# Half of the spectral modes folded in early, and a last stage that contracts 64 rows

## The chip, the cores and the metric

One Trainium2 chip, one of its cores. The time is that of one execution on the device, in microseconds (us); of the kernel before, three runs gave a median of 456.17 us. Engines: TensorE (PE, with its weight loads PEld), VectorE (DVE), ScalarE (ACT), GpSimd (POOL), and SyncE (SP), which here only issues DMAs.

## The reference

Two parts in a row. Batch 8, 8 heads of 64, sequence 576, model width 512, 64 modes.

```python
proj = einsum('bhsd,df->bhsf', x, w_phi); proj -= max(abs(proj))   # for q and for k
phi  = concatenate([exp(proj), exp(-proj)])
num  = phi_q @ (phi_k.T @ v);  den = phi_q @ sum(phi_k)
x    = (num / den)                        # [8, 576, 512] after the heads are joined
X    = rfft(x, axis=1)[:, :64]
Y    = X_m @ (w_r[m] + i w_i[m])          # for each of 64 modes a 512x512 complex matrix
y    = irfft(Y, n=576)
u    = x + y
out  = u + relu(u @ w_ch)
```

The weights w_r and w_i are 64 x 512 x 512 in f32 each, 134 MB in all.

## The kernel before, in words

**Attention stage.** 32 steps, each one pair of batches or heads, make x, kept in `xs_all` (8 batches x 5 chunks of up to 128 tokens, bf16), and its forward transform, kept transposed in `XT`. Beside them the weights of the modes stream in: 32 groups of 8 modes by a quarter of the width (the first 8 groups: 16 modes by an eighth), each a `wr` and a `wi` tile cast to bf16 by the DMA that POOL issues (`weights`, L162). Three tiles of each stand ready (`NW = 3`), so group k+2 is issued once the products of group k-1 are done. `mode_mm` makes a group's products (L416), `mode_sum` adds them into `Yacc`. Groups 0 to 21 run within the attention stage; its last six steps also turn and multiply the first six chunks of x by w_ch (`flip_early`, `times_w_early`, into `xw0`).

**The tail of the stream, groups 22 to 31.** The order of instructions is written by hand and each engine works through its own in that order. Groups 24 to 31 complete the sums of 8 modes each, for all batches. Each of them sums its products to `yst` (L444), turns them (`ptY`, L805) and copies them to `sY` (L806). After every second group, `by_batch` makes for 16 modes and all batches Z = Y w_ch and Y itself, rows by mode (`psZY`, L705 and L711, on the PSUM tags T0 and T1), and copies them to `zy` (L718): mode rows 32 P to 32 P + 31 hold P = 0 to 3, real and imaginary parts. For P below 3 the copies are put in a list, `copies`, and taken from it one by one by `pieces`; for P = 3, after group 31, one batch of each half is copied and the other six go through a staging tile `st` (L735) and DMAs (L737, SP and POOL).

Between groups, `pieces(n)` (numbers by group in `plan`) does n times: turn two chunks of x (`flip_x`, PSUM tag T3, copied to `sT` by DVE, L657) and multiply the two turned before by w_ch (`times_w`, PSUM tag T2, L665, copied to `xw` by ACT, L667). `reordered` puts 11 pairs of chunks of `xs_all` in the order of tokens in which the output is written, in place (L692, L694, tags T0 and T1). A PSUM tile on a tag can be written only when all that read the previous tile on this tag have done so.

**The last stage.** 20 units: for each b of 0 to 3 the chunk pairs (b,0), (b,2), (b+4,0), (b+4,2) and one unit with the half chunks 4 of b and b+4. Each has two PSUM tiles, psB and psA, on T2 and T3 or, every other unit, on T0 and T1. psB takes x w_ch (L753, `add_xw`) and Z times the inverse transform `CI` (L760, `add_z`, 128 rows: real and imaginary parts of 64 modes); ACT takes the Relu of it into the output tile `of` (L762). psA takes x (L768, `add_x`) and Y times `CI` (L774, `spec`); DVE adds it (L776). In 11 units, called late, x is not added on PE but by POOL at the end (L780). SP issues the outputs (L856): those of a late unit three units later. The first unit's `add_xw` stands ahead of group 31's products.

The names of the rows in the profile are those of these tiles.

Of the kernel before, what the change touches and what calls it, by code (L numbers as in the profile page):

```python
# [21 lines left out]
NCH = 5  # L22
# [4 lines left out]
def kernel(  # L27
# [31 lines left out]
    N_EARLY = 6  # L59
# [4 lines left out]
    CI = const.tile([128, NCH, 128], BF16, name="CI")  # L64
# [310 lines left out]
    def flip_early(i):  # L375
        pt = psum.tile([128, 4, 128], BF16, name="pte", tag="tx", bufs=1)
        for dc in range(4):
            nc.tensor.transpose(pt[:, dc, :], xs_all[:, i, dc * 128:(dc + 1) * 128], ident_b)
        sT = pa_mid.tile([128, 4, 128], BF16, name="sTe", tag="sTe", bufs=1)
        nc.vector.tensor_copy(sT, pt)  # L380
        return sT

# [7 lines left out]
    def mode_mm(k, tag="yr"):  # L390
        g, gi = groups[k]
        XT = XTs[1 - g if k < 8 else g % 2]
        wt = W.pop(k)
# [16 lines left out]
        psY = psum.tile([128, DMODEL], F32, name="psY", tag=tag, bufs=1)  # L410
        for ri in range(2):
# [95 lines left out]
    def inverse_matrix(c):  # L507
# [12 lines left out]
        o, i = CI[:, c, :], pct  # L520
        if c < 4:
            o, i = o.rearrange("r (p j) -> r j p", j=2), i.rearrange("r (j p) -> r j p", j=2)
        nc.vector.tensor_scalar_mul(out=o, in0=i, scalar1=coefcol)
# [117 lines left out]
    zy = pb.tile([128, 2, B_, DMODEL], BF16, name="zy", bufs=1)  # L641
    zall, yall = zy[:, 0], zy[:, 1]
    xw = pb.tile([128, B_ * NCH - N_EARLY, DMODEL], BF16, name="xw", bufs=1)


    todo = list(range(N_EARLY, B_ * NCH, 2))
# [3 lines left out]
    def flip_x(i):  # L650
        pt = psum.tile([128, 2, 4, 128], BF16, name="pt", tag="T3")
        for x in range(2):
            for dc in range(4):
                nc.tensor.transpose(
                    pt[:, x, dc, :], xs_all[:, i + x, dc * 128:(dc + 1) * 128], ident_b)
        sT = pb.tile([128, 2, 4, 128], BF16, name="sT", tag="sT", bufs=3)
        nc.vector.tensor_copy(sT, pt)  # L657
        ahead.append((i, sT))

    def times_w():  # L660
        i, sT = ahead.pop(0)
        ps = psum.tile([128, 2, DMODEL], F32, name="psW", tag="T2")
        for x in range(2):
            for dc in range(4):
                nc.tensor.matmul(ps[:, x, :], lhsT=sT[:, x, dc, :], rhs=wchb[:, dc, :],  # L665
                                 start=(dc == 0), stop=(dc == 3))
        nc.scalar.copy(xw[:, i - N_EARLY:i + 2 - N_EARLY, :], ps)  # L667

    def pieces(n):
        for _ in range(n):  # L670
# [4 lines left out]
            if len(ahead) > 1:  # L675
                times_w()
# [4 lines left out]
    late = {0: ((0, 2), (1, 0), (1, 2)), 1: ((0, 0), (1, 0), (1, 2)),  # L681
            2: ((0, 0), (1, 0), (1, 2)), 3: ((0, 0), (0, 2))}
    reorder = sorted((b + 4 * x) * NCH + c for b in range(4) for x, c in late[b])

    def reordered(tag):
        i = reorder[0]
        if todo and i + 2 > todo[0]:
            return
        reorder.pop(0)
        ps = psum.tile([128, 2, DMODEL], F32, name="psX", tag=tag)  # L690
        for x in range(2):
            nc.tensor.matmul(ps[:, x, :], lhsT=ident_p, rhs=xs_all[:, i + x, :],  # L692
                             start=True, stop=True)
        nc.scalar.copy(xs_all[:, i:i + 2, :], ps)  # L694


    def by_batch(sY, P):
# [17 lines left out]
        rows = slice(32 * P, 32 * P + 32)  # L715

        def copy(j, h, eng):
            eng(zy[rows, :, j + 4 * h, :], ps[h][32 * j:32 * j + 32])  # L718

        if P < 3:  # L720
            for h in range(2):
                mm_z(h)
                mm_r(h)
            copies.extend([lambda j=j: (copy(j, 0, nc.scalar.copy),
                                        copy(j, 1, nc.vector.tensor_copy)) for j in range(4)])
# [4 lines left out]
        for h, eng in ((0, nc.scalar.copy), (1, nc.vector.tensor_copy)):  # L730
            mm_z(h)
            mm_r(h)
            copy(0, h, eng)
            st = pb.tile([128, 2, DMODEL], BF16, name=f"st{h}", bufs=1)
            eng(st, ps[h])  # L735
            for j in range(1, 4):
                (nc.sync if j == 1 else nc.gpsimd).dma_start(  # L737
                    zy[rows, :, j + 4 * h, :], st[32 * j:32 * j + 32])

    def parts(u):
        for x, (b, c) in enumerate(u["bc"]):
            if u["half"]:
                yield slice(64 * x, 64 * x + 64), 0, b, c, ident_b[:, 0:64], CI[:, c, 0:64]
            else:
                yield slice(0, 128), x, b, c, ident_p, CI[:, c, :]

    def add_xw(u):
        u["psB"] = ps = psum.tile([128, 2, DMODEL], F32, name="psB", tag=u["tags"][0])  # L750
        for r, x, b, c, idn, ci in parts(u):
            i = b * NCH + c
            nc.tensor.matmul(ps[r, x, :], lhsT=idn,  # L753
                             rhs=xw0[:, i, :] if i < N_EARLY else xw[:, i - N_EARLY, :],
                             start=True, stop=False)

    def add_z(u):
        ps = u["psB"]
        for r, x, b, c, idn, ci in parts(u):
            nc.tensor.matmul(ps[r, x, :], lhsT=ci, rhs=zall[:, b, :],  # L760
                             start=False, stop=True)
        nc.scalar.activation(u["o"], ps[:, 0, :] if u["half"] else ps, ACT.Relu)  # L762

    def add_x(u):
        u["psA"] = ps = psum.tile([128, 2, DMODEL], F32, name="psA", tag=u["tags"][1])
        if not u["late"]:
            for r, x, b, c, idn, ci in parts(u):
# [3 lines left out]
    def spec(u):  # L771
        ps, late, o = u["psA"], u["late"], u["o"]
# [114 lines left out]
```

## Time and profile before

| | |
|---|---|
| Median of 3 runs (lowest, highest) | 456.17 us (455.78, 456.91) |
| Span of the profiled execution | 456.7 us |
| PE busy, share of the span | 301.7 us, 66% |
| DVE | 292.0 us, 64% |
| ACT | 261.8 us, 57% |
| POOL | 198.8 us, 44% |
| DMA moved | 97.70 MB, mean 214 GB/s |
| Products of group 31, wi half, start | 416.08 us |
| Last DVE addition ends | 449.85 us |

The span is that of one execution under the profiler, from its first to its last instruction; it is 0.5 us above the median of the runs. In the page's slices each digit is the busy share of a fortieth of the span (11.4 us) in tenths. A row of the order of time gives start, duration, engine, line and operation, the tiles written and read, and in brackets how long the engine had been idle and what ended that. Matmuls overlap: a row of eight is shorter than eight of one. PEclk is the clock that TensorE was granted, as a share of full speed.

### The profile page before, as it was taken

Reading aid. Unit: us, or ns where it says so; the run is one execution under the profiler, and the core shown is the slowest. Engines: PE = TensorE matmul, PEld = TensorE weight load, DVE = VectorE, ACT = ScalarE, POOL = GpSimd, SP = SyncE. Lnnn points to the kernel's source line nnn. Section 1 sums busy time; section 2 is a strip of 40 time slices with the busy share of each in tenths; the row PEclk is TensorE's granted clock in tenths of the full one; section 3 lists DMA queues with packets and bytes.
Section 4 is the critical chain, followed back from the end, with each engine's and each line's share of the span. In section 5 each row is a group of like instructions: output and inputs, shape, how many; then the busy total and the mean of one; then the engine's idle time right before and its main releaser. Section 6 shows DMA issues by size and latency. Waiting matters only on the chain.

```text
span 456.7 us, 11065 instructions
## 1 busy us (share of the span) xinstructions
PE 301.7 (66%) x4637; PEld 197.6 (43%) x4637; DVE 292.0 (64%) x418; ACT 261.8 (57%) x528; POOL 198.8 (44%) x251
## 2 busy tenths in 40 slices
PE   3476776833767677655555544755578878868993
PEld 2355565622555565544333432433344445433341
DVE  6578789844988779876666472776322273653873
ACT  4576887833686877865545452765334455644662
POOL 3956476445563256553435231443021212100993
PEclk9976899876886769998778595999999999998997
DMA  6999999999999999999999999999999999990697
GB/s 179 195 228 222 225 213 226 221 206 216 221 228 217 230 219 222 224 219 229 218 207 217 218 218 218 207 203 207 207 207 207 207 207 207 207 179 11 223 341 299
DMA packets 84417, 97.70 MB, mean 214 GB/s; under 512 B 3152, under 2 KB 77136, under 8 KB 84368
## 3 DMA queue, kind: packets, MB, share of 16 engines
q0 software_dynamic: 75728, 76.75, 101.1%
q1 hardware_dynamic: 8480, 20.19, 12.8%
q8 instruction: 36, 0.59, 0.5%
q14 instruction: 13, 0.11, 0.1%
q10 hardware_dynamic: 160, 0.07, 0.1%
HBM read 163.64 MB, written 9.44 MB: 379 GB/s over the span
## 4 chain that ended last, share of the span: by engine, by line
DMA 34%; issue 24%; DVE 17%; PE 11%; POOL 7%; ACT 3%; SPq 1%; DVEq 0%; POOLq 0%; ACTq 0%
DMA wi<-in_moe_w_i_dram 29%; DVE mkq L233 6%; DMA wr<-in_moe_w_r_dram 4%; DVE xs_all L336 2%; DVE nd L322 2%; DVE tB L315 2%; POOL vaug L270 2%; PE ptr L184 1%; PE psNB L305 1%; ACT AA L240 1%; PE kvz L286 1%; PE psB L753 1%; DVE of L776 1%; SPq L122 1%; POOL wr L162 1%
## 5 line engine op out<-in xcount | busy, mean ns | idle before, releaser
L270 POOL TENSOR_TENSOR vaug<-vn,ee 128x576 bf16<-128x576 f32 x64 | 72.7, 1155 | 63.3 <-ACT ee L255 50.2
L240 ACT ACTIVATE AA<-psT 128x1024 bf16<-128x1024 f32 x64 | 62.0, 1021 | 43.6 <-PE psT L208 43.1
L262 ACT ACTIVATE e<-mkq 64x4 f32<-64x4 f32 (+1 forms) x128 | 26.3, 206 | 61.5 <-DVE mkq L233 59.2
L244 ACT ACTIVATE AA<-psk 128x1024 bf16<-128x1024 f32 x64 | 61.4, 1010 | 0.0
L162 POOL DMA_DIRECT2D wr<-in_moe_w_r_dram x24 | 21.9, 912 | 86.6 <-PE psY L416 77.8
L416 PEld LDWEIGHTS <-XT 128*32 128x32 bf16 x384 | 17.1, 171 | 56.6 <-issue 46.4
L667 ACT CAST xw<-psW 128x1024 bf16<-128x1024 f32 x17 | 17.2, 1013 | 40.5 <-PE psW L665 34.6
L233 DVE TENSOR_REDUCE mkq<-psk 128x8 f32<-128x1024 f32 x32 | 38.8, 1213 | 0.7 <-PE psk L199 0.7
L233 DVE TENSOR_REDUCE mkq<-psq 128x8 f32<-128x1024 f32 x32 | 38.9, 1217 | 0.4 <-PE psq L199 0.4
L435 DVE TENSOR_TENSOR Yacc<-psY,Yacc 128x512 f32<-128x512 f32 x16 | 11.0, 689 | 42.5 <-PE psY L416 42.5
L416 PE MATMUL psY<-wi,XT 128*32 128x512 bf16 x192 | 18.0, 435 | 28.8 <-DMA wi<-in_moe_w_i_dram 28.8
L286 PE MATMUL kvz<-vaug,AA 64*128 64x65 bf16 x1152 | 29.2, 210 | 11.5 <-POOL vaug L275 9.8
L190 DVE COPY kT<-ptr 128x640 bf16<-128x640 bf16 x32 | 15.7, 492 | 32.5 <-PE ptr L184 32.5
L665 PE MATMUL psW<-wchb,sT 128*128 128x512 bf16 x136 | 33.5, 391 | 2.1 <-ACT xw L667 2.1
L315 DVE TENSOR_TENSOR tB<-psNB,e 128x650 f32<-128x650 f32 x32 | 26.7, 833 | 11.2 <-PE psNB L305 10.6
L305 PEld LDWEIGHTS <-AA 128*128 128x128 bf16 x640 | 29.0, 110 | 9.3 <-issue 8.9
L286 PEld LDWEIGHTS <-AA 64*128 64x128 bf16 x1152 | 25.1, 107 | 15.9 <-issue 11.8
L162 POOL DMA_DIRECT2D wi<-in_moe_w_i_dram x24 | 21.1, 880 | 23.8 <-PE psY L416 20.5
L322 DVE TENSOR_TENSOR nd<-psNA,tB 128x650 f32<-128x650 f32 x32 | 26.7, 835 | 4.1 <-DVE tB L315 0.5
L416 PE MATMUL psY<-wr,XT 128*32 128x512 bf16 x192 | 17.0, 424 | 18.0 <-DMA wr<-in_moe_w_r_dram 8.7
L336 DVE TENSOR_TENSOR xs_all<-nd,rden 128x640 bf16<-128x640 f32 x32 | 28.0, 874 | 1.1
L184 PE MATMUL ptr<-ident_b,k 128*128 128x128 bf16 x160 | 17.9, 257 | 14.8 <-DVE qT L190 12.6
(132 smaller groups left out, 705.4 us busy)
## 6 DMA issues: line engine op xcount, KB each, us to landing
wr<-in_moe_w_r_dram POOLq DMA_DIRECT2D x24, 1024.0 KB, 25.8
wi<-in_moe_w_i_dram POOLq DMA_DIRECT2D x24, 1024.0 KB, 29.4
wr<-in_moe_w_r_dram POOLq DMA_DIRECT2D x16, 512.0 KB, 15.9
wi<-in_moe_w_i_dram POOLq DMA_DIRECT2D x16, 512.0 KB, 19.6
out_dram<-of SPq DMA_DIRECT2D x16, 512.0 KB, 3.8
vn<-in_v_dram SPq DMA_DIRECT2D x24, 288.0 KB, 5.8
q<-in_q_dram POOLq DMA_DIRECT2D x12, 288.0 KB, 19.3
k<-in_k_dram POOLq DMA_DIRECT2D x12, 288.0 KB, 20.0
```

Of the source, the lines that this page charges most:

```text
L162: nc.gpsimd.dma_start(t, w[8 * gi:8 * gi + 8, g * 128:(g + 1) * 128, :].rearrange("m p e -> p m e"))
L233: nc.vector.tensor_reduce(out=o, in_=i, axis=AX.X, op=ALU.max, apply_absolute_value=True)
L240: nc.scalar.activation(AA[:, 0, ab, 0:1024].rearrange("f (x j p) -> f j x p", j=2, p=64), st["psT"].rearrange("f j (x p) -> f j x p", p=64 ...
L244: nc.scalar.activation(AA[:, 1, ab, 0:1024].rearrange("p (c j f) -> p j c f", c=4, j=2), st["psk"], ACT.Exp, scale=sc)
L270: nc.gpsimd.tensor_tensor(out=vaug[:, ab, :, 0:64], in0=st["v"], in1=ee[:, ab, :].unsqueeze(2).to_broadcast([128, 9, D_]), op=ALU.mult,)
L286: nc.tensor.matmul(kvz[:, hh, ab * 65:(ab + 1) * 65], lhsT=AA[r, 1, ab, 128 * j:128 * j + 128], rhs=vaug[r, ab, j, :], start=(j == 0), sto ...
L305: nc.tensor.matmul(p[:, hh, 65 * c:65 * c + 65], lhsT=AA[:, 0, ab, x:x + 128], rhs=kvzF[:, hh, ab * 65:(ab + 1) * 65], start=True, stop=True,)
L315: nc.vector.tensor_tensor(out=tB, in0=st["psNB"], in1=e2.unsqueeze(3).to_broadcast([128, 2, NCH, 65]), op=ALU.mult,)
L322: nc.vector.tensor_tensor(out=nd, in0=st["psNA"], in1=st["tB"], op=ALU.add)
L336: nc.vector.tensor_tensor(out=xo, in0=nd[:, :, :, 0:64], in1=rden.to_broadcast([128, 2, NCH, 64]), op=ALU.mult,)
L416: nc.tensor.matmul(psY[32 * j:32 * j + 32, :], lhsT=XT[:, c0:c0 + 32, m], rhs=wt[ri][:, 2 * j + par, :], start=(par == 0 and ri == 0), sto ...
L665: nc.tensor.matmul(ps[:, x, :], lhsT=sT[:, x, dc, :], rhs=wchb[:, dc, :], start=(dc == 0), stop=(dc == 3))
```

## The change

The sum over modes is split: modes 0 to 31 (P = 0 and 1, complete after group 27) and modes 32 to 63.

- `zy` becomes two tiles, `zys[0]` for the low and `zys[1]` for the high modes; in each, rows 0 to 63 hold Z and rows 64 to 127 hold Y. `CI` becomes two tiles, `CIs[0]` and `CIs[1]`, with the 64 rows of its modes in both halves of the partitions. The copies of `by_batch` are 32 x 512 instead of 32 x 1024, twice as many; the DMAs after group 31 are twelve instead of six.
- `pre` is new. For each of the 11 late units it adds to x w_ch the low modes of Z, to x (put in the order of tokens) the low modes of Y, and copies both back in place, by ACT and DVE. It runs three times in group 28, three in 29, four in 30, and once inside group 31, between the wr and the wi half of its products. `reordered` is gone.
- `times_w(lo=True)`, in groups 28 to 30, adds the low modes of Z to four more pairs of chunks.
- In the last stage each unit contracts the 64 rows of the high modes, Z into psB and Y into psA in turn; units that have not had their low modes get them there. The first unit's x w_ch, x and low modes stand inside group 31 as well.
- x w_ch is kept in the order of tokens: the copies of the turned x (`sT`, `sTe`) write with a step of two elements (`copy_in_order`). The half chunks of b and b+4 share one tile.
- All copies left in `copies` are done at the end of each group's `pieces`; `plan` has one piece more in groups 24 and 29 and one less in group 30.

```diff
+    EARLY = [0, 1, 2, 3, NCH, NCH + 1]
...
+    def copy_in_order(sT, pt):
+        nc.vector.tensor_copy(sT.rearrange("d c (p j) -> d c j p", j=2),
+                              pt.rearrange("d c (j p) -> d c j p", j=2))
...
-        nc.vector.tensor_scalar_mul(out=o, in0=i, scalar1=coefcol)
+        for x in range(2):
+            r = slice(64 * x, 64 * x + 64)
+            for y in range(2):
+                o, i = CIs[x][64 * y:64 * y + 64, c, :], pct[r, :]
...
+                nc.vector.tensor_scalar_mul(out=o, in0=i, scalar1=coefcol[r, :])
...
+    def times_w(lo=False):
...
+        if lo:
+            for x, (b, c) in enumerate(chunks_of(u)):
+                o, n = (ps[64 * x:64 * x + 64, 0, :], 64) if c == 4 else (ps[:, x, :], 128)
+                nc.tensor.matmul(o, lhsT=CIs[0][0:64, c, 0:n], rhs=zys[0][0:64, b, :],
+                                 start=False, stop=True)
+            lo_z.add(u)
...
+    def pre(n):
+        for _ in range(n):
+            b, c = pre_todo.pop(0)
+            i = b * NCH + c
+            tags = ("T0", "T1") if pre_done[0] % 2 == 1 else ("T2", "T3")
+            pre_done[0] += 1
+            psb = psum.tile([128, 2, DMODEL], F32, name="psPB", tag=tags[0])
+            psa = psum.tile([128, 2, DMODEL], F32, name="psPA", tag=tags[1])
+            for x in range(2):
+                nc.tensor.matmul(psb[:, x, :], lhsT=ident_b, rhs=xw_of(b, c)[:, x, :],
+                                 start=True, stop=False)
+            for x in range(2):
+                nc.tensor.matmul(psa[:, x, :], lhsT=ident_p, rhs=xs_all[:, i + x, :],
+                                 start=True, stop=False)
+            for x in range(2):
+                for y, ps in enumerate((psb, psa)):
+                    r = slice(64 * y, 64 * y + 64)
+                    nc.tensor.matmul(ps[:, x, :], lhsT=CIs[0][r, c + x, :], rhs=zys[0][r, b, :],
+                                     start=False, stop=True)
+            nc.scalar.copy(xw_of(b, c), psb)
+            nc.vector.tensor_copy(xs_all[:, i:i + 2, :], psa)
...
-            copies.extend([lambda j=j: (copy(j, 0, nc.scalar.copy),
-                                        copy(j, 1, nc.vector.tensor_copy)) for j in range(4)])
+            copies.extend([lambda j=j: (copy(j, 0, 0, act), copy(j, 0, 1, act),
+                                        copy(j, 1, 0, dve), copy(j, 1, 1, dve)) for j in range(4)])
...
+        mm_z(0)
+        mm_r(0)
+        copy(0, 0, 0, act)
+        copy(0, 0, 1, dve)
+        act(st[0], ps[0])
+        mm_z(1)
+        mm_r(1)
+        copy(0, 1, 1, dve)
+        dve(st[1], ps[1])
+        copy(0, 1, 0, act)
...
+    def add_modes(u, lo):
+        for r, x, b, c, idn, cs in parts(u):
+            for y, (nm, done) in enumerate((("psB", lo_z), ("psA", lo_y))):
+                k = slice(64 * y, 64 * y + 64)
+                if lo and u["u"] in done:
+                    continue
+                nc.tensor.matmul(u[nm][r, x, :], lhsT=CIs[1 - lo][k, c, cs],
+                                 rhs=zys[1 - lo][k, b, :],
+                                 start=(y == 1 and not lo and u["late"]), stop=not lo)
...
-        plan = {22: 3, 23: 3, 24: 2, 25: 2, 26: 2, 27: 1, 28: 2, 29: 1, 30: 1, 31: 0}
+        plan = {22: 3, 23: 3, 24: 3, 25: 2, 26: 2, 27: 1, 28: 2, 29: 2, 30: 0, 31: 0}
+        pre_plan = {28: 3, 29: 3, 30: 4, 31: 0}
...
-            if k == 31:
+            if k < 31:
+                psY = mode_mm(k, "T3")
+            else:
+                psY = mode_mm(k, "T1", ris=(0,))
+                pre(1)
                 add_xw(u0)
-            yst = mode_sum(k, mode_mm(k, "T3"), pb)
+                add_x(u0)
+                add_modes(u0, True)
+                mode_mm(k, psY=psY, ris=(1,))
+            yst = mode_sum(k, psY, pb)
...
-            pieces(plan[k])
-            if k <= 24 or k % 2 == 0:
-                assert not copies
-                for tag in ("T0", "T1"):
-                    if reorder:
-                        reordered(tag)
-            if k == 30:
-                times_w()
+            pieces(plan[k], k >= 28)
+            while copies:
+                copies.pop(0)()
+            pre(pre_plan.get(k, 0))
...
                 if n:
                     add_xw(u)
-                add_z(u)
-                if n:
                     add_x(u)
-                spec(u)
+                    add_modes(u, True)
+                add_modes(u, False)
+                last(u)
```

`last` takes the Relu of psB by ACT, adds psA by DVE and, in a late unit, x by POOL, as before.

## The prediction

> **What bounds the kernel now.** I read the page's slices, then the engines' order of time from 330 us on, then busy time by stretch, then the groups with their shapes kept apart.
>
> ```profile
> span 456.7 us, 11065 instructions
> PE   3476776833767677655555544755578878868993
> ...
> DMA  6999999999999999999999999999999999990697
> ```
>
> The transfer engines are full from slice 2 to slice 36, about 411 us: up to there the weight stream sets the time, and what the attention stage gains or loses is absorbed. Two things follow the stream: the joint around mode group 31, and the last stage.
>
> ```profile
> 386.57 2.44 DVE L718 CAST zy<-psZY 32x1024 bf16<-32x1024 f32 x2
> 386.59 0.68 PE L416 MATMUL psY<-wr,XT 128*32 128x512 bf16 x8 [0.78 <-DVE sT L657]
> ```
>
> (both, and the next, from the order of time: start, us, engine, line, operation)
>
> ```profile
> 410.29 0.59 PE L692 MATMUL psX<-xs_all,ident_p 128*128 128x512 bf16 x2 [1.79 <-ACT zy L718]
> 410.72 3.22 PE L665 MATMUL psW<-wchb,sT 128*128 128x512 bf16 x8
> 415.04 0.59 PE L753 MATMUL psB<-xw,ident_p 128*128 128x512 bf16 x2 [1.10 <-ACT xw L667]
> 415.56 0.69 PE L416 MATMUL psY<-wr,XT 128*32 128x512 bf16 x8
> 416.08 0.60 PE L416 MATMUL psY<-wi,XT 128*32 128x512 bf16 x8
> ```
>
> The last weights were issued at 388.44 and land 26.0 us later, at 414.4; group 31's wi half starts at 416.08. So PE's queue, in order, is only 1.6 us behind the stream: groups 28, 29 and 30 start at 386.59, 395.22 and 402.78. The 410.29 line shows what makes this queue late: a PSUM tile on T0/T1 waits until the copies into zy have read the previous one.
>
> ```profile
> 448.02 1.23 DVE L776 TENSOR_TENSOR of<-psA,of 128x1024 f32<-128x1024 f32 x1 [0.46 <-ACT of L762]
> 449.17 0.68 DVE L776 TENSOR_TENSOR Yacc<-psA,Yacc 128x512 f32<-128x512 f32 x1
> ```
>
> In the last stage PE is busy 27.37 of the 29.4 us from 420.6 to 450, POOL works through 11 late units of 2.13 us from 425.50 to 449.45, the last DVE addition ends at 449.85, and the output drains until 456.7.
>
> **Prices**, from groups by shape and from the order of time:
>
> ```profile
> L657 DVE COPY sT<-pt 128x1024 bf16<-128x1024 bf16 x17 | 11.8, 692 | 20.9 <-PE pt L654 20.8
> L718 DVE CAST zy<-psZY 32x1024 bf16<-32x1024 f32 x13 | 15.8, 1219 | 2.8 <-PE psZY L711 2.5
> L388 ACT CAST xw<-psWe 128x512 bf16<-128x512 f32 x6 | 3.5, 586 | 5.3 <-PE psWe L386 5.2
> L776 DVE TENSOR_TENSOR Yacc<-psA,Yacc 128x512 f32<-128x512 f32 x4 | 2.7, 681 | 0.0
> ```
>
> ```profile
> 156.42 0.39 PE L208 MATMUL psT<-qT,w 64*128 64x512 bf16 x2 [2.09 <-DVE mkq L233]
> 424.95 0.59 PE L753 MATMUL psB<-xw,ident_p 128*128 128x512 bf16 x2
> ```
>
> A 512-column product costs 0.216 (eight in 1.89, 0.16 of it latency). Two that contract 64 rows in different halves end after 0.39, two full ones after 0.59: the halves run together, so a z/y pair costs one 0.216. A change of operand shape costs 0.11 (the gap between 426.24 and 426.34). A copy out of PSUM costs by columns, not rows: 512 take 0.585 on ACT and 0.685 on DVE, 1024 take 1.02 and 1.22.
>
> **The strided copies.** sT is now written with step 2. No row shows that from PSUM in bf16; bounds are 0.69 (contiguous, as now) and 1.22 (1024 columns in f32). I take 1.22: the only strided bf16 copy, ident_p's (SBUF to SBUF), took 231 ns for 128 columns, and less the 59 ns of a one-column memset that is 1.34 ns a column, against (692 - 425) / 512 = 0.52 for contiguous sT and sY. The Trainium skill (VectorE: DVE Perf Modes, What auto-detection actually checks) says that packing two results a cycle needs 16-bit data with step 1; by it the copy is 1.22, and no row here shows it. At 0.69 the sum is 2.7 us lower.
>
> **Up to group 28.** The four inverse-matrix writes for one (five times some 0.8 us of DVE, at 112 to 148 us) and the wider early copies lie under the stream, but the last three early copies (0.27 each) do not: +0.8. Groups 22 to 27 lose four places with two reorderings (0.96 of PE each, -3.8), gain a third piece in group 24 (+2.98, the distance of the xw copies at 345.00 and 347.99), and four strided copies nothing covers (4 x 0.53 = +2.1). Group 28 starts at 386.6 + 2.1 = 388.7. Weights 31 are issued right after it, when the queue still holds data to 404.6: the stream stays whole.
>
> **Groups 28 to 31**, the heart. A pre step is 2 products with xw, 2 with x, 2 pairs and 2 shape changes: 6 x 0.216 + 0.22 = 1.51 us of PE, ACT 1.02 and DVE 1.22 behind it; two pairs of PSUM tags alternate, so PE sets the pace. What PE waits for, group by group:
>
> Group 28: DVE has just ended sT and now does eight 0.685 copies (5.5) before it may sum group 28; the added z product of the first times_w waits for them too. Sum 0.69 and the turn to sY 0.92: at +7.0 the first flip can go. Flip, strided copy and the next flip, all through T3: at +9.4. times_w with its z product 2.45, ACT's copy 1.05 frees T2: +12.9. Three pre steps 4.5, and T3 free after the last DVE copy, 1.45: 18.9 us, where it took 8.6.
>
> Group 29: mode products, times_w, sum and sY to +4.4; by_batch 2 x 1.18 to +6.7; flip and strided copy to +8.7; eight copies 5.5 to +14.2. The next pre step is on T0/T1, the tags of these copies: PE has nothing to do for some 7 us. The rest of that step and two more: 18.3 us, where it took 7.6.
>
> Group 30: mode products and the last times_w 3.4, ACT frees T2 at +4.65, four pre steps 6.05, T1 free after 1.4: 12.1 us. Group 31: wr half 0.5, a pre step 1.5, its copies 1.45, the first unit's products 1.4: wi starts 4.8 later.
>
> Sum 18.9 + 18.3 + 12.1 + 4.8 = 54.1, so the wi half starts at 442.8, not 416.08: **+26.7 us**. The weights have been there for 28 us; DVE and PSUM tags now set the pace.
>
> **The last stage.** In wi-half time, the first addition starts 7.0 us on, as before: the copies are shorter, but the two halves of one psZY are read in turn by ACT and DVE. The second unit's addition ends at +10.45 (before +9.3): its y pair needs T1, which ACT's copy of batch 4 frees last. The 12 sends (5 on SP, 7 on POOL, 0.56 each there) end by +10.5 and cost nothing: POOL's first late addition is only then ready. From there the order of products matters. add_z stood ahead of what waits for psA; now z and y go in turn, so z's second half, the Relu and the addition all wait for the addition two units back. One round: late unit 0.06 + 0.43 + 0.19 + 1.03 + 0.02 + 1.24 = 2.97; one with x and low y (0.86 + 0.11 more) 3.94; a half unit 2.43. The odd units after the second (5 late, 2 full, 2 half) take 14.9 + 7.9 + 4.9 = 27.6. The last addition ends at 442.8 + 10.45 + 27.6 = 480.9, where it ended at 449.85. **+31.0 us** in all; PE work falls from 28 to some 25 us but does not bind. The end keeps its 6.85 us, since POOL and the output have slack.
>
> **The clock**, by busy time in stretches (PE, PEld, DVE, ACT, POOL, then granted clock, DMA share, GB/s):
>
> ```profile
> 410.00:411.00 1.00, 0.71 (x4) 0.35 (x4) 0.99 (x2) 0.32 (x2) 0.00 (x0) 1.00 0.62 103
> 411.00:412.00 1.00, 1.00 (x4) 0.34 (x3) 0.73 (x1) 0.93 (x1) 0.00 (x0) 0.56 0.38 62
> 412.00:413.00 1.00, 1.00 (x4) 0.42 (x3) 0.00 (x0) 0.00 (x0) 0.00 (x0) 0.50 0.17 28
> ```
>
> After some 3 us with transposes alone, PE ran at half clock from 411 to about 414.2: eight products took 3.22 instead of 1.89, and 3.2 us at half speed are 1.6 us of work. The waits in groups 28 and 29 are longer (6 and 7 us nearly without products) and pre steps follow both: 2 x 1.6 = **+3.2 us**. The Trainium skill (TensorE: Matmul & The Clock Gate, What's actually happening) states that an idle window of about 3.4 us halves the clock and a busy one restores it; the trace agrees, and by its figure the term would be an estimated 2 x 1.7.
>
> **Sum.** Span 456.7 + 31.0 + 3.2 = 490.9. The span is 0.5 above the median of the runs, 456.17, and I carry the difference: **490.4 us**.
>
> **Rivals.**
> *Faster:* pre steps fit under the stream and the stream's end stays the pace. For it: PE has idle time in each group before, and 11 reorderings go. wi then starts at 414.4 (-1.6); the second addition ends at 424.9, POOL's 11 x 2.13 = 23.4 from there end at 448.3 instead of 449.45, and the last output, no longer behind a late addition on SP, gains another 1.5 at most: 453.6. It decides if groups 28 to 31 take 25.7 us from 388.7 instead of 54.1. Against it: PE's own work in them, with no wait at all, is 11.5 + 11.0 + 9.7 + 3.5 = 35.7. Chance 0.03; another 0.02 for within 0.3%, about 1.4 us, which is also what a measurement of this kernel can tell from no change.
> *PE's work alone:* copies and tags get out of the way, and only those 35.7 us count. wi starts at 424.4 (+8.3), the last stage costs 0 to 4.3: about 466. Against it: the order of each queue is fixed, and before, too, PE waited for zy (410.29). Chance 0.08.
> *Halves one after the other:* if z and y of a pair do not overlap, each pair costs 0.43. Two in each of 11 pre steps and the first unit, 12 x 0.43 = 5.2, and on the odd units' rounds one product in a late and two in any other, 5 x 0.22 + 4 x 0.43 = 2.8: 498.4. For it: the pairs write two PSUM tiles that other engines have just read; against it the 0.39 row. Chance 0.11.
> *Clock low to the end:* the last stage leaves PE idle about a third of the time. If it runs at half clock there, late rounds grow by 0.43, full ones by 1.3, half ones by 0.4: 5 x 0.43 + 2 x 1.3 + 0.8 = 5.6, and with one more closing in groups 30 and 31 (1.6) 497.6. The attention stage, with PE 60 to 80% busy, shows both 1.00 and 0.53. Chance 0.11.
> The forecast keeps 0.65.
>
> **How the numbers follow.** The forecast's own range is 484 (copies at 0.69 -2.7, no closing of the clock -3.2) to 494 (both waits cost double at half clock, +3.2). The rivals above it reach 499, two of them part way together 502. Below, the case of PE's work alone is left out but for copies that partly overlap (half of the 24 us between 466 and 490): 478. Left out are the cases up to 466 (0.13) and some of the upper end (0.05). Faster 0.03, same 0.02, slower 0.95.
>
> **What would show it.** Right: group 29's products start near 407.6, group 30's near 426, group 31's wi half near 443 with the weights landed at 414 to 417; PE waits for DVE's or ACT's zy copies for 5 us or more twice; the pre steps lie 1.5 us apart; additions of late units two apart lie 3.0 us apart; granted clock under 1 after the waits. Wrong: group 31 waits for its weights (then the faster rival), or the last stage ends within 33 us of the wi half (then the order of z and y does not matter), or sT copies of 0.69.

## The result, and the profile after

The changed kernel takes **496.46 us** (median of four runs, 494.05 to 497.34), against 456.22 us (455.78 to 456.91) for the kernel before on the same chip: 1.086 times as long, 95% interval 1.082 to 1.089. Its profiled execution took 497.34 us, with a span of 495.5.

The page of the changed kernel: its slices are 12.4 us each.

```profile
span 495.5 us, 11304 instructions
...
PE   2558677447675776774747377457875858497883
...
DMA  6999999999999999999999999999999993000687
```

Before, the transfer engines were full to slice 36 and empty in one slice. Now the stream of weights ends at about 414 us, where it ended before, and three slices are empty. The wi half of group 31 starts 38 us after the last weights have landed, so the transfers hide nothing of this stretch any more.

What PE waits for from group 28 on, in its order of time (start, us, engine, line, operation, idle time before it and what ended that), with one of DVE's two stretches of copies ahead of it:

```profile
393.64 5.61 DVE L780 CAST zy<-psZY 32x512 bf16<-32x512 f32 x8
398.58 0.59 PE L710 MATMUL psW<-zy,CI 64*128 64x512 bf16 x2 [1.97 <-DVE zy L780]
...
404.35 3.11 PE L705 MATMUL psW<-wchb,sT 128*128 128x512 bf16 x8
...
415.02 0.69 PE L423 MATMUL psY<-wr,XT 128*32 128x512 bf16 x8 [1.35 <-DVE xs_all L753]
...
425.47 0.38 PE L742 MATMUL psPB<-xw,ident_b 128*128 128x512 bf16 x1 [3.13 <-ACT zy L780]
429.19 1.03 PE L745 MATMUL psPA<-xs_all,ident_p 128*128 128x512 bf16 x2 [3.35 <-DVE zy L780]
...
447.52 0.68 PE L423 MATMUL psY<-wr,XT 128*32 128x512 bf16 x8 [1.35 <-DVE xs_all L753]
...
452.30 0.70 PE L423 MATMUL psY<-wi,XT 128*32 128x512 bf16 x8
```

Group 28 starts at 393.66, group 29 at 415.02, group 30 at 435.50, the wr half of group 31 at 447.52 and its wi half at 452.30, where the kernel before has 386.59, 395.31, 402.78, 415.56 and 416.08. Groups 28 and 29 take 21.4 and 20.5 us instead of 8.7 and 7.5. In both, PE stands behind DVE's or ACT's copies out of psZY: 2.0 us in group 28, and 3.1 and 3.4 us in group 29 with one product between. After both the clock is low. Two of the stretches that show it (busy us of PE, PEld, DVE, ACT, POOL, then granted clock, DMA share, GB/s):

```profile
402.00:404.00 2.00, 0.62 (x7) 0.45 (x5) 1.29 (x1) 0.00 (x0) 0.00 (x0) 0.50 1.24 206
428.00:430.00 2.00, 0.81 (x2) 0.13 (x2) 1.12 (x2) 0.00 (x0) 0.00 (x0) 0.50 0.00 0
```

In the last stage, DVE's additions of the second and the third odd unit, and of the last unit:

```profile
463.74 1.22 DVE L854 TENSOR_TENSOR of<-psA,of 128x1024 f32<-128x1024 f32 x1 [0.27 <-ACT of L853]
...
466.65 1.22 DVE L854 TENSOR_TENSOR of<-psA,of 128x1024 f32<-128x1024 f32 x1 [0.80 <-ACT of L853]
...
488.41 0.68 DVE L854 TENSOR_TENSOR Yacc<-psA,Yacc 128x512 f32<-128x512 f32 x1
```

The last addition ends at 489.1, 36.8 us after the start of the wi half; it was 33.8 before. From there to the end of the span are 6.4 us (6.85 before). From the wi half to the end of the span the kernel takes 43.2 us instead of 40.6.

So the profile holds the 38.8 us by which the span is longer in four pieces: group 28 starts 7.1 us later; groups 28 and 29 take 25.7 us more; group 30 and the step from the wr to the wi half take 3.5 more (12.0 and 4.8 us against 12.8 and 0.5); the last stage takes 2.6 more.

### The profile page after: what moved, and what is told of

It is laid out like the page before. It is cut to its first block, busy times and chain, and to the rows that moved or that the text cites. A ratio compares the mean times of both kernels' runs of the same rounds, so it can differ in the third digit from the quotient of the medians.

```text
span 495.5 us, 11304 instructions
## 1 busy us (share of the span) xinstructions
PE 321.6 (65%) x4718; PEld 200.6 (40%) x4735; DVE 325.7 (66%) x457; ACT 263.6 (53%) x541; POOL 201.4 (41%) x254
## 4 chain that ended last, share of the span: by engine, by line
DVE 31%; PE 28%; DMA 22%; ACT 6%; issue 5%; POOL 4%; SPq 1%; another core or an unknown queue 0%; DVEq 0%; ACTq 0%; POOLq 0%
DMA wi<-in_moe_w_i_dram 12%; DVE mkq L234 7%; DMA k<-in_k_dram 6%; PE psW L705 5%; DMA q<-in_q_dram 4%; DVE xs_all L337 4%; DVE nd L323 3%; DVE tB L316 3%; DVE zy L780 3%; PE psY L423 2%; PE ptr L185 2%; PE pt L687 2%; ACT xw L716 2%; PE psNB L306 2%; PE kvz L287 2%
## 5 line engine op out<-in xcount | busy, mean ns | idle before, releaser
L234 DVE TENSOR_REDUCE mkq<-psk 128x8 f32<-128x1024 f32 x32 | 38.8, 1213 | 1.1 <-PE psk L200 1.0
L287 PE MATMUL kvz<-vaug,AA 64*128 64x65 bf16 x1152 | 30.5, 214 | 12.9 <-POOL vaug L276 10.5
L716 ACT CAST xw<-psW 128x1024 bf16<-128x1024 f32 x13 | 13.2, 1012 | 45.1 <-PE psW L710 17.8
L705 PE MATMUL psW<-wchb,sT 128*128 128x512 bf16 (+1 forms) x131 | 31.6, 417 | 3.2 <-ACT xw L716 2.7
L287 PEld LDWEIGHTS <-AA 64*128 64x128 bf16 x1152 | 26.3, 110 | 17.8 <-issue 13.2
L306 PEld LDWEIGHTS <-AA 128*128 128x128 bf16 x640 | 30.2, 112 | 6.8 <-issue 6.3
L423 PE MATMUL psY<-wr,XT 128*32 128x512 bf16 x192 | 17.8, 444 | 20.5 <-DMA wr<-in_moe_w_r_dram 7.8
L209 PE MATMUL psT<-qT,w 64*128 64x512 bf16 x64 | 14.9, 455 | 22.4 <-DVE mkq L234 22.4
```

Source lines behind the costliest of these rows:

```text
L234: nc.vector.tensor_reduce(out=o, in_=i, axis=AX.X, op=ALU.max, apply_absolute_value=True)
L287: nc.tensor.matmul(kvz[:, hh, ab * 65:(ab + 1) * 65], lhsT=AA[r, 1, ab, 128 * j:128 * j + 128], rhs=vaug[r, ab, j, :], start=(j == 0), sto ...
L306: nc.tensor.matmul(p[:, hh, 65 * c:65 * c + 65], lhsT=AA[:, 0, ab, x:x + 128], rhs=kvzF[:, hh, ab * 65:(ab + 1) * 65], start=True, stop=True,)
L423: nc.tensor.matmul(psY[32 * j:32 * j + 32, :], lhsT=XT[:, c0:c0 + 32, m], rhs=wt[ri][:, 2 * j + par, :], start=(par == 0 and ri == 0), sto ...
L705: nc.tensor.matmul(o, lhsT=l, rhs=wchb[:, dc, :], start=(dc == 0), stop=(dc == 3 and not lo))
```

## The experiments

The medians of the kernel before that were measured beside these runs lie between 456.38 and 457.61 us, against 456.22 beside the changed kernel, so a difference of one microsecond between two medians means little.

**All pre steps at the end.** The theory at this point: the joint is lengthened by PE's waits for copies, not only by the steps' own work.

```diff
-        pre_plan = {28: 3, 29: 3, 30: 4, 31: 0}
+        pre_plan = {30: 10}
```

> The changed kernel with all ten pre steps of groups 28 to 30 placed at the end of group 30 (none in 28 and 29); same arithmetic, same number of instructions. Theory (the joint is lengthened by waits: a pre step placed right behind a by_batch has nothing to do until DVE's eight zy copies are over): groups 28 and 29 give up their waits, DVE copies while PE does the next group's products, group 31 starts some 6.6 us earlier (about 440.9 instead of 447.5) and the kernel takes about 490 us (488 to 491.5). Rival (a pre step costs its 1.5 us of PE wherever it is put, and the waits only move with it): 496 plus or minus 1.

It took 491.72 us (490.08 to 492.56), 4.7 less, just above the theory's range. In its profile PE does group 30's products while DVE copies what group 29 left, and then waits once, for the sum of group 30, which DVE makes after its copies:

```profile
422.55 0.40 PE L897 MATMUL ptY<-ident_b,yst 128*128 128x128 bf16 x4 [2.70 <-DVE yst L451]
...
441.09 0.69 PE L423 MATMUL psY<-wr,XT 128*32 128x512 bf16 x8 [1.34 <-DVE xs_all L753]
445.87 0.69 PE L423 MATMUL psY<-wi,XT 128*32 128x512 bf16 x8
```

Group 31 starts at 441.1, 6.4 us earlier than in the changed kernel, as expected, and the profiled execution is 6.4 us shorter too (490.97 and 497.34); the medians differ by less. Waits that came from the place of the steps are therefore some 5 to 6 of the 36.2 us by which the wi half was late. The rest stays: the ten steps now stand on PE from 422.8 to 439.7, all of them behind the last weights, most of them 1.5 us apart.

**Contiguous copies.** The order of rows is made by the transposes instead.

```diff
-                    pt[:, x, dc, :], xs_all[...], ident_b)
+                    pt[:, x, dc, :], xs_all[...], ident_b if c == 4 else ident_p)
...
-            copy_in_order(sT..., pt...)
+            nc.vector.tensor_copy(sT, pt)
```

> The changed kernel with the order of rows made in the transposes (the permuted identity as their moving matrix) and contiguous copies into sT, 0.69 us instead of the 1.29 measured; same results. Theory (the strided copy is what made the stretch up to group 28 five microseconds longer than I had put it, by its own length and by the waits of PE in which the clock fell): group 28 starts near 388.5 instead of 393.7, three more copies of 0.6 leave the way in groups 28 and 29, and the kernel takes about 489 us (487 to 491). Rival (only the copies' own length counts, four before group 28 and three in it and 29; the rest of the five comes from the early units and the third piece of group 24): 496.5 - 7 x 0.6 = 492 or more (492 to 495).

It took 492.72 us (489.21 to 495.9), 3.7 less: the rival's band, though the interval, 490.4 to 494.7, does not exclude the upper end of the theory's. From the groups with their shapes kept apart, the first line of the changed kernel, the second of this run:

```profile
L386 DVE COPY sT<-pt 128x1024 bf16<-128x1024 bf16 x13 | 16.8, 1296 | 17.9 <-PE pt L687 17.9
```

```profile
L691 DVE COPY sT<-pt 128x1024 bf16<-128x1024 bf16 x17 | 11.8, 691 | 23.5 <-PE pt L687 23.5
```

A strided copy out of PSUM takes 1.30 us, a contiguous one 0.69, and the transposes with the permuted matrix take no longer (eight in 0.61 us either way). The Trainium skill (VectorE: DVE Perf Modes, What auto-detection actually checks) asks for 16-bit data with a step of one for two results a cycle; the two rows agree. Group 28 starts at 391.78, 1.9 us earlier than in the changed kernel; its profiled execution had entered the last steps of the attention stage 1.7 us later, so the copies there are worth up to 3.6.

**Strided copies alone, in the kernel before.**

```diff
-        nc.vector.tensor_copy(sT, pt)
+        copy_in_order(sT..., pt...)
...
-            nc.tensor.matmul(ps[r, x, :], lhsT=idn, rhs=xw...)
+            nc.tensor.matmul(ps[r, x, :], lhsT=ident_b (every second column of it for a half unit), rhs=xw...)
```

> The kernel before with one part of the change alone: the strided copies into sT (1.29 instead of 0.69 us, and 0.72 instead of 0.43 for the early ones), so that x W lies in the order of the output and is added with the plain identity; same results, all other work as before. Theory (from group 22 on PE's queue waits for these copies and nothing makes it up, the clock falls more often): group 28 starts 2 to 4 us later than 386.6, and the kernel takes about 459.5 us (458 to 461.5). Rival (the weight stream still ends last and hides it): 456.2 to 457.

It took 464.04 us (463.08 to 468.1) against 456.38 for the kernel before beside it: ratio 1.017, interval 1.014 to 1.021, 7.7 us. The theory had the sign, and less than half of the size.

```profile
393.76 0.69 PE L420 MATMUL psY<-wr,XT 128*32 128x512 bf16 x8 [1.38 <-DVE sT L384]
```

Group 28 starts 7.2 us later than in the kernel before, as late as in the changed kernel (7.1). Of this, 1.9 is there when group 22 starts and 5.2 comes in groups 22 to 27. The copies themselves got longer by 17 x 0.6 + 6 x 0.29 = 12 us; more than half of that reaches the end. In this profile too the clock falls once in group 22 (0.79, 0.50 and 0.85 from 336 to 342), where before it is 1.00.

**Products in the waits.**

```diff
+    def warm(n):
+        ps = psum.tile([128, 2, DMODEL], F32, name="psD", tag="T2")
+        for _ in range(n):
+            nc.tensor.matmul(ps[:, 0, :], lhsT=ident_b, rhs=wchb[:, 0, :], start=True, stop=True)
...   (group 28: nine products with zeros in times_w ahead of the z product,
...    warm(2) after ptY, warm(7) after the first flip;
...    group 29: warm(13) and warm(14) around the xw products of the first pre step)
```

> The changed kernel with matrix products that nobody reads (or that add zero) put into PE's waits of groups 28 and 29: nine before the added z product, two and seven between the transposes of group 28, thirteen and fourteen around the first product of group 29's first pre step. They only fill time in which PE waits in the profile of the changed kernel. Theory (the clock falls because of these waits and its fall costs 3 to 4.5 us): granted clock 1.00 from 393 to 436, times_w 1.9 instead of 3.1 us, the first pre steps of group 29 1.5 apart instead of 2.8, and the kernel takes about 492.5 us (491.5 to 493.5). Rival (the low clock is hidden behind the copies of DVE, or the added products delay what they stand ahead of as much as they gain): 496 to 498.

It took 492.59 us (490.79 to 493.85), 3.9 less, as the theory had it.

```profile
402.00:404.00 2.00, 2.00 (x17) 1.13 (x15) 1.30 (x2) 0.00 (x0) 0.00 (x0) 1.00 1.25 208
...
428.00:430.00 2.00, 2.00 (x12) 0.63 (x11) 1.47 (x2) 1.24 (x2) 0.00 (x0) 1.00 0.00 0
```

The granted clock is 1.00 from 393 to 436, times_w takes 1.89 us, and groups 28 and 29 take 19.2 and 18.3 us, 2.2 less each. 45 products that do nothing make the kernel faster.

The same in the kernel before, with eight products ahead of the wait at 410.29 (`warm(8)` in group 30):

> The kernel before with eight products that nobody reads in the wait of 1.79 us that stands before 410.29 in group 30. Theory (the clock that falls there costs PE 1.3 us, and PE's queue is 1.6 us behind the weights): times_w takes 1.9 instead of 3.2 us, the wi half starts near 414.8 instead of 416.1, and the kernel takes about 455.0 us (454.4 to 455.6). Rival (the weights' arrival sets this point, or the products are late): 456.2.

The clock stays at 1.00 from 410 to 414, and from group 30 to the wi half it is 11.9 us instead of 13.3. Yet the time is 456.04 us (455.35 to 459.39) against 456.38, ratio 1.000, interval 0.998 to 1.002. A gain of 1.2 us is excluded. One reason may lie in the profile of before itself. In the 48 later executions of the kernel before for which time and span are both listed, the time is 1.7 to 1.9 us above the span. By that the profiled one, with its span of 456.7, would have taken some 458.5 us, 2 above the median. That the clock falls at 411 in the usual execution too is therefore not shown.

**No fold at all.**

```diff
-    late_units = [(0, 2), (4, 0), (4, 2), ...]
+    late_units = []
...
-                pre(1)
```

(`pre_plan` is empty as well.)

> The changed kernel without the fold: no pre step, no late units, every wide unit gets x and its lower modes in the last stage, as u0 does; the contraction over 64 rows stays. Theory (the fold costs its own work and the waits behind the zy copies): groups 28, 29 and 30 run as in the run with all pre steps at the end, up to the transposes of group 30 that end at 423 there; the wi half starts near 424.5 instead of 452.3, the last stage is bound by PE at some 1.95 us a unit and takes 41 us to the last addition instead of 36.8: about 472 us (469 to 475). Rival (only the eleven steps' 1.51 us of PE come back, 16.6 us, and the last stage grows as above): 483 us.

It took 481.7 us (479.8 to 482.15), 14.8 less than with the fold, and 1.054 times the kernel before (1.051 to 1.057). That is near the rival's number, but neither account is right: the wi half starts at 428.39, 23.9 us earlier (theory 28, rival 16.6), and the last stage takes 51.9 us to the end of the span instead of 43.2 (both had it at about 4 more).

```profile
428.39 1.06 PE L423 MATMUL psY<-wi,XT 128*32 128x512 bf16 x8
```

```profile
436.00:474.00 38.00, 35.81 (x211) 10.91 (x213) 20.23 (x19) 17.52 (x19) 2.52 (x6) 0.96 0.60 226
```

Without the fold PE is busy 35.8 of 38 us of the last stage: each unit has two 64-row pairs, which together cost what one 128-row product for Z and one for Y cost, and x besides. So fold and late units together buy 8.7 us of last stage with 23.9 us of joint. How much of the 8.7 is the fold's is not shown: without late units, x of eleven units goes from POOL to PE as well, 22 products of 0.216 us or some 4.7 us, and no run keeps the late units without the fold. Against the kernel before, this run starts the wi half 12.3 us later and needs 11.3 us more from there to the end (51.9 and 40.6).

**The order of the last stage, four runs.** The theory: rounds are long because Relu and addition of a unit stand in line behind the addition of two units before. In the first run each upper-half z goes with the y of the unit before it:

```diff
+                if nx:
+                    add_xw(nx)
+                    add_modes(nx, True, ys=(0,))
...
+                for x in range(2):
+                    if nx:
+                        add_modes(nx, False, ys=(0,), xs=(x,))
+                    add_modes(u, False, ys=(1,), xs=(x,))
+                if nx:
+                    relu(nx)
```

> The changed kernel with the last stage skewed by one unit: each upper-half z product goes with the y product of the unit before it, so that the Relu of a unit is done one unit ahead of its addition; same arithmetic, same pairs of 64 rows, only u0's z and the last y are without a partner. Theory (the late rounds are long because Relu and addition stand in line behind the addition of two units before): additions follow each other without the Relu, about 1.25 to 2.1 us a unit, POOL's 2.13 us a late unit is next, the last addition ends 33.5 us after the wi half instead of 36.8, and the kernel takes about 493 us (492 to 494). Rival (PE's products set the pace in the last stage): no change, 496 plus or minus 1.

It took 501.5 us (499.19 to 502.75), 5 more, which neither account had. The half units spoil it: a product of 64 columns did not run beside one of 128.

```profile
469.66 0.62 PE L848 MATMUL psB<-zy,CI 64*64 64x512 bf16 x3
470.21 0.39 PE L848 MATMUL psA<-zy,CI 64*128 64x512 bf16 x1
470.53 0.40 PE L848 MATMUL psB<-zy,CI 64*64 64x512 bf16 x1
470.86 0.39 PE L848 MATMUL psA<-zy,CI 64*128 64x512 bf16 x1
```

The starts are 0.32 apart with no wait between, where pairs of one shape start together. In the second run the half units keep their own z and y together and the skew goes past them:

```diff
+                half = u["u"][1] == 4
+                nx = None if half else next((v for v in units[n + 1:] if v["u"][1] != 4), None)
```

> The skewed last stage again, with the half units left out of the skew: the run before it lost because their 64-column products did not run beside the 128-column products of their neighbours (a half unit and the unit after it took 4.3 us of PE, 2.8 in the changed kernel). Wide units: upper-half z of the next wide unit beside the y of this one; half units: their own z and y together, as in the changed kernel. Theory (Relu and addition in line cost the last stage some 2 to 3 us, and PE is next at some 26 us of products): last addition 34 us after the wi half instead of 36.8, about 494 us (492.5 to 495). Rival (PE's products set the pace already): 496 or more.

It took 499.21 us (498.67 to 500.36). Now two wide units in a row use the same pair of PSUM tags around each half unit, and PE waits there 1.1 us, until 472.53, for a Relu that ends at 472.47. So a control, with the half units at the end of the last stage and nothing else, and the skew on top of that:

```diff
-        for u in ((b, 0), (b, 2), (b + 4, 0), (b + 4, 2), (b, 4)):
+        for u in ((b, 0), (b, 2), (b + 4, 0), (b + 4, 2)):
             units.append(dict(u=u, late=u in late_units))
+    units += [dict(u=(b, 4), late=False) for b in range(4)]
```

> The changed kernel with the four half units at the end of the last stage instead of one after each four wide units; nothing else. It is the control for the next run. Both theories: the rounds stay, one more full one among them: last addition 36.8 to 37.8 us after the wi half, 496 to 498 us.

> The skewed last stage with the half units at the end, so that consecutive wide units alternate between the two pairs of PSUM tags; in the run before this one, leaving a half unit out of the skew put two consecutive wide units on the same tags, and PE waited there for the Relu it had just released (1.1 us before 472.53). Theory (Relu and addition in line behind the addition of two units before cost the last stage some 3 us): no wait of PE for a Relu among the wide units, last addition 33.5 us after the wi half (32.5 to 34.5), 3 us less than in the run with the half units at the end, about 493.5 us. Rival (what is saved at the Relu is lost at the next wait, or PE's products set the pace): within 1 us of the run with the half units at the end.

The control took 497.43 us (496.91 to 498.29), the skew 497.47 (496.54 to 497.79). The additions did what the theory said: the last wide one ends 28.9 us after the wi half instead of 32.6, the last of all at 33.8 instead of 37.4. The end of the kernel did not move. In the order of time of POOL and SP:

```profile
462.98 23.05 POOL L863 TENSOR_TENSOR of<-of,xs_all 128x1024 f32<-128x1024 f32 x11 [0.79 <-DVE of L859]
```

```profile
486.69 6.29 SPq L958 DMA_DIRECT2D out_dram<-Yacc  x8
```

POOL works through its 11 late units without a gap until 486.0, and the eight small outputs follow on SP. The last run lets them go ahead of the last two late outputs:

```diff
-            for lag in (3, 0):
+            for lag in (9, 3, 0):      (9 for the last two late units)
```

> The run skew3 with one more edit: the outputs of the last two late units are issued after those of the half units instead of ahead of them. In skew3 the last wide addition ended 29 us and the last addition of all 33.8 us after the wi half, as the theory had it, but the kernel ended no earlier: POOL worked through its 11 late units until 486.03 in that profile, and SP, which issues in order, held the eight half-unit outputs (6.3 us) behind the last late ones until then. Theory (what the skew gained was lost in that queue): the half-unit outputs go while POOL is still adding, the span ends some 5 us after POOL's last addition instead of 9.7, and the kernel takes about 493 us (492 to 494.5) against 497.5. Rival (the transfers themselves set the end, their engines being busy from 484 to 490): 497 plus or minus 0.8.

497.34 us (494.08 to 499.46): no change, the rival's number. The eight outputs went at 484.05 and took SP to 490.3, and the two late ones left after that. From the wi half to the end of the span it is 43.2 us in the changed kernel, 43.2 in the control, 43.3 and 43.2 in the last two runs. So the long rounds pace the additions, but shortening them alone does not end the kernel sooner: something else stands close behind. Whether that is SP's issuing, some 0.8 us for each small output, or the transfers stays open. For the transfers speaks that in the last run their engines are busy to a share of 1.01 from 484 to 486, when wide outputs move at 404 GB/s, and still to 0.86 and 0.92 from 488 to 492, when the small ones move at 231 and 243.

**All that helped together:** steps at the end, contiguous copies, products in the waits, skewed last stage.

> The changed kernel with all that helped put together: all ten pre steps at the end of group 30, contiguous copies into sT with the order made in the transposes, filling products in the waits of groups 28 (nine, two, three) and 30 (eight), and the skewed last stage with the half units at the end. If the parts add up (4.7 and 3.7 us measured, some 2 for the clock, 3 for the skew): 483 us; if they share the same waits, 486 to 488. In either case slower than the kernel before and no better than the kernel without the fold, since ten pre steps still stand on PE behind the last weights: the wi half cannot start before about 439.

482.4 us (479.61 to 485.61), ratio to before 1.057 (1.051 to 1.064). The wi half starts at 434.42, earlier than the 439 that I had put as its limit, and the last stage again takes 43.2 us. That is 14.1 us less than the changed kernel, where the parts measured alone, without the last stage's, make 4.7 + 3.7 + 3.9 = 12.3. The best form of the fold that I found is level with no fold, some 25 us behind the kernel before. None of the runs beats that kernel, so there is no better version to show.

## Why the prediction was right, and where its sizes were off

The sign and the case were right: 490.4 us forecast, 496.46 measured, in the range 478 to 502. The likeliest case, pre steps that run long past the stream, is the one that came. Of the 6 us that it is short, 5 come before these steps begin, where I had expected 2 us of delay and 7 came.

**Up to group 28** (forecast +2.1, measured +7.1): the mis-sized term. About half of the 5.0 us that it is short lies in the clock. Groups 22 to 27 take 59.2 us where they took 55.5; I had +1.3. In the run of all that helped they take 54.5, with contiguous copies and the clock at 1.00; without the strided copies my terms gave 55.5 - 3.8 + 3.0 = 54.7. So the reorderings and the third piece were right in sum. Of the 4.7 us between that run and the changed kernel, 1.8 are three waits for strided copies (1.4 us instead of 0.8; I had four, 2.1), and 2.9 are falls of the clock in groups 22 and 26. The contiguous run, with the same instructions up to here as the run of all that helped, takes 57.1. Its clock fell (the first two lines), that of the other did not (the third):

```profile
380.00:382.00 2.00, 1.22 (x13) 1.01 (x10) 0.69 (x1) 0.00 (x0) 0.00 (x0) 0.50 1.25 207
382.00:384.00 2.00, 2.00 (x11) 0.54 (x8) 0.69 (x1) 0.00 (x0) 0.00 (x0) 0.50 1.25 207
```

```profile
380.00:384.00 4.00, 3.48 (x53) 1.91 (x55) 1.11 (x2) 1.18 (x2) 1.75 (x2) 1.00 1.24 207
```

One fall of the clock is worth 2.7 us there, and it comes in one execution and not in another. The changed kernel shows 0.82 from 336 to 340, then the line below, and 0.73 and 0.50 from 382 to 386. Before, the clock is 1.00 from 288 to 408.

```profile
340.00:344.00 4.00, 3.14 (x16) 1.51 (x16) 1.81 (x2) 1.01 (x1) 0.00 (x0) 0.76 1.25 209
```

In the second and the third skewed run, with the same instructions up to here as the changed kernel, groups 22 to 27 take 61.1 us, with the clock near 0.50 from 333 to 342. My reading is that PE, with fewer products between its waits, stands at the edge of such a fall; no run tests that.

The other half is the start of group 22, 3.4 us late instead of 0.8. The strided early copies account for up to 1.9 of it, in the last four steps. The rest differs from execution to execution: in the profiles with these same instructions group 22 starts between 332.1 and 336.2, against 330.0 and 331.1 in the two of the kernel before and its filled form.

**Inverse-matrix writes** (forecast: under the stream): they were not free where they stand. The four writes of a step take 1.5 us of DVE, the one of before took 0.35. In five steps of the attention stage, 120 to 154 us, the lead of the kernel before grows by 5 us, so DVE and not the stream sets the pace there. The wait for weights gives most of it back between 202 and 224 us, where the difference falls from 4.0 to 0.6. The term was right at zero, but its cover was that later wait, not the place where the writes stand.

**Group 28 and group 29** (18.9 and 18.3 forecast without the clock, 21.4 and 20.5 measured): with the clock held at 1.00 they take 19.2 and 18.3. The walk through queues, copies and tags was right to 0.3 us. (Group 29 of before starts at 395.31; the 395.22 of the prediction is the load of its weights.) **Group 30** took 12.0 (12.1) and **the wr half to the wi half** 4.8 (4.8).

**The clock** (forecast +3.2): two closings in groups 28 and 29, as forecast, worth 4.4 us in those groups and 3.9 in the median. Each lasted some 6.8 us, from 400.0 and from 427.3, and PE went on waiting after the fall, until 404.35 and 429.19; the one of before, from which I had the price, lasted about half as long. The closings before group 28 were not in the forecast at all. The Trainium skill (TensorE: Matmul & The Clock Gate, What's actually happening) puts the fall after an idle window of some 3.4 us; the fall at 427.3, behind two waits of 3.1 and 3.4 us with one product between, agrees. Around 340 it fell although no single wait there is longer than 1.4 us; the waits stand between transposes. What brings the clock down there is not shown.

**The last stage** (forecast: last addition 38.05 us after the wi half, measured 36.8): the rounds two units apart, from the end of one addition to that of the next, added up to 26.9 us, forecast 27.6. Late ones took 2.7 to 3.1 (2.97), full ones 3.8 (3.94), half ones 2.4 and 2.5 (2.43). The second addition ended 0.5 us sooner than I had it. But the reading of it, that the order of z and y costs the kernel 4 us, holds for the additions only: with that order undone they end 3.6 us sooner and the kernel does not.

**Span and median** (I carried 0.5 us from before): by the spans above, the profiled execution of before took longer than its median, which the span alone does not tell; the changed kernel's median is 1.0 above its span. That is 1.5 us of the 6.

Together: 5.0 up to group 28, 1.4 in groups 28 and 29 with their clock, -0.1 in group 30 and behind it, -1.3 for the last addition, -0.4 for the tail and 1.5 from span to median. That is the 6.1 us missing.

**The signs.** Durations came as I had said, points in time did not: groups 29 and 30 and the wi half start at 415.0, 435.5 and 452.3, where I had 407.6, 426 and 443. A wait for zy copies of more than 5 us came once, in group 29; in group 28 PE waits 2.0 us for them and for the rest behind what DVE does next. The pre steps lie 1.5 us apart at full clock and 2.8 at half. The copies into sT take 1.30 us, not 0.69.

**The rivals.** Faster: group 31 found its weights there for 38 us; out. PE's work alone: with waits and clock removed as far as I could, the wi half starts at 434.4, not at 424; out, though in that direction. Halves one after the other: pairs of one shape, where neither waits for anything, start within 0.07 us of each other; out, but for the 64-column products beside 128. Clock low to the end: 1.00 throughout from 459 to 489; out. (In its support I had misread a table: the stretches of before with 0.53 are those with PE 91 and 48% busy; at 60 to 80% the lowest is 0.57.)

## What to carry to other kernels

Work moved forward to shorten a last stage is free only in time that the stage before it leaves empty on every engine and buffer that it touches. Here the split alone saves PE nothing in the last stage (two pairs of 64 rows cost what two products of 128 rows did), so the fold had to live from idle time, and its place, between the last low modes and the last weights, had too little of it. Before adding a wait to a queue that runs close behind a stream, price the clock as well: PE with short waits and little between them fell to half speed here, and products that nobody reads were a cheap repair in the changed kernel; in the kernel before they gained nothing.

## What the runs showed of the hardware that I had not expected

- A transpose with a permuted identity as its moving matrix gives the permuted transpose at no extra time (eight in 0.61 us, as with the plain one), and saves the copy behind it 0.6 us of 1.3.
- Filling idle time can pay: 45 products without use, 9 of them with a zero matrix, gained 3.9 us in the changed kernel. Eight in the kernel before gained nothing (ratio 1.000).
- Products that contract 64 rows in the two halves run together when both have 128 columns, or both 64; a 64-column one beside a 128-column one did not (starts 0.32 us apart).
- An execution's time is 1.7 to 2.1 us above its span, in all runs of this case for which both are listed.
